# A planned attention and gated-unit kernel: new planner costs, reciprocal and product apart, products of two taps also on GpSimd

## The chip, the cores and the metric

The kernel runs on one core of a Trainium2 chip. The core has five engines that run side by side: TensorE (PE in the tables, its weight loads PEld), VectorE (DVE), ScalarE (ACT), GpSimd (POOL), and SyncE (SP), which here issues all transfers. Each engine works its own queue in order. Matmul results land in PSUM, eight banks; GpSimd's operands in this kernel all lie in SBUF. The metric is the device time of one launch in microseconds.

## What is computed

Eight batches of causal attention with a learned decay (8 heads, 576 positions, 64 per head), and on their result a gated linear unit with a causal convolution of five taps as its gate (conv_w is 5 x 512):

```python
scores = scale * np.matmul(q, k.transpose(0, 1, 3, 2))
s_pos = np.maximum(s, 0.0)
cum = np.cumsum(s_pos, axis=-1)
bias = -(cum[:, :, :, None] - cum[:, :, None, :])
scores = np.where(causal, -1000000000.0, scores + np.minimum(bias, 0.0))
...
attn = attn / (np.sum(attn, axis=-1, keepdims=True) + 1e-09)
return np.matmul(attn, v).astype(np.float32)
...
x = np.ascontiguousarray(attn_out.transpose(0, 2, 1, 3)).reshape(B, S, H * D)
...
K = conv_w.shape[0]
...
for k in range(K):
    gate_pre += conv_w[k][None, None, :] * xp[:, k:k + S, :]
gate = 1.0 / (1.0 + np.exp(-gate_pre))
val = x @ w_val
return (gate * val @ w_out).astype(np.float32)
```

## The kernel before, in words

The work is cut into 32 pieces `n`, four pairs of heads in each of eight batches; a pair of heads is also a block of 128 channels of the gated unit. For one piece:

- q and k are loaded (SP), cast to bf16 (the tiles qb and kb), transposed (PE, L524) and copied out of PSUM (QKT, L528, ACT or DVE). The last 64 positions of all heads go a way of their own (tail, tailb, L513, L516).
- V is multiplied by its decay weight w (Vp, L495), with a column of w beside it that later gives the sum of the row.
- Scores in three steps (PE, L533), each followed by an exp on ACT over 128x1024 (P, L559); the diagonal blocks of the first step are masked on POOL (L565), the last block apart (L545, L570).
- The product with V (PE, L580), a reciprocal of the sums (DVE, L586) and the normalisation (DVE, L587) give xn, which PE transposes (L595). An evacuation (L599, ACT or DVE) makes xT in SBUF.
- The convolution of this block: a first product, x times the weight of tap 0 (L395 on ACT, L397 on DVE or POOL), then four taps on DVE (L609), each adding a shifted product to gp in place, 575, 574, 573 and 572 columns wide. DVE and ACT read x from PSUM, POOL reads xT. A tanh (ACT, L614) ends it.
- Once the four xT blocks of a batch are there, PE makes val in halves of 288 columns (L621), DVE multiplies it into the gate (glu, L627), PE multiplies with w_out (L633), ACT or DVE copies the result out of PSUM (ot, L638), and SP stores it.

No order is written out. Every step is handed to a planner (`Plan`) with its engine, a duration, a due time made from the table `DUE`, and what it needs, takes and gives back (PSUM banks, and a few SBUF buffers: three P, two gp, six th, three ot, three qkf). Where more than one engine can do a step, a digit in the table `CHOICE` says which. `run` then plays the engines against each other with these durations: whenever an engine is free, it starts the ready step with the lowest due time. The order in which steps start is the order in which they are emitted, and so the order of every queue. A result is taken to reach another engine 0.2 us after its step ends (`LAG`), and its own engine at once:

```python
for o in after[t["n"]]:
    o["at"] = max(o["at"], t["done"] + (self.LAG if o["eng"] != e else 0.0))
```

A last step counts whether all reciprocals were in range (`check_recs`, `count`); if not, a general path would run. It does not here.

Of the kernel before, what the change touches and what calls it, by code (L numbers as in the profile page):

```python
# [2 lines left out]

# [201 lines left out]
def pcol(kb, qb):  # L205
    if kb == qb:
        return kb * 128
    if qb == 4:
# [13 lines left out]

DUE = dict(w=-9.02, lwv=-0.69, lwo=-0.63, cwv=-14.48, cwo=12.35, av=1.54, norm=-21.42, xt=-10.52, xe=-5.49,
           tap=4.19, dtap=-0.1, tanh=-21.1, val=6.51, dval=0.82, out=13.05, dout=0.32, oute=12.26,
           qt=-3.29, qe=62.47, tt=-0.65, te=-32.14, s4=-6.89, vp=-31.92, cast=41.14, lqk=-6.48,
           mask=-32.97, lv=-68.98)

STAY = (0.33, 20.6)  # L230

CHOICE = dict(cast="22212012",
              wts="00",
              te="10100110",
              qe="10010001000100000100100000000000",
              xe="01000110000001000110100110101101",
              tap0="10200210102212220121120122002000",
              oute="1010000010101000001000010000100000100000")


class Plan:

    LAG = 0.2
    SWITCH = 0.18

    def __init__(self, bufs):
# [14 lines left out]
    def run(self):  # L263
# [33 lines left out]
        while len(self.order) < len(self.tasks):  # L297
            started, later = False, []
            for e in engs:
# [50 lines left out]
                later.append(idle_at[e])  # L350
                started = True
                for o in after[t["n"]]:
                    o["at"] = max(o["at"], t["done"] + (self.LAG if o["eng"] != e else 0.0))
                    o["left"] -= 1
                    if o["left"] == 0:
                        ready[o["eng"]].append(o)
# [6 lines left out]
def main_path(ctx, tc, q, k, v, s, moe_w_val, moe_conv_w, moe_w_out, out, okcnt):  # L363
# [53 lines left out]
    xns = two("xn", [128, NKB, 512], BF16)  # L417
    xTs = two("xT", [128, 4, S], BF16)
    glus = two("glu", [128, 4, S], BF16)
    sp = one.tile([64, S], FP32, name="sp")  # L420
    cum = one.tile([64, S], FP32, name="cum")
    chalf = one.tile([64, 1], FP32, name="chalf")
# [35 lines left out]
    for m, (nm, src, dst, sc) in enumerate((("wv", moe_w_val, wv, 1.0), ("wo", moe_w_out, wo, 0.5))):  # L458
        def load(nm=nm, src=src):
            wt = slot[nm] = work("qkf", nm, [128, 4, DM], FP32)  # L460
            nc.sync.dma_start(out=wt, in_=src.rearrange("(c p) d -> p c d", c=4))
        t = add("SP", 3.6, DUE["l" + nm], load, take=[("qkf", nm)])
# [110 lines left out]
    def av(n, hh):  # L573
        b, p = divmod(n, 4)
        ps = slot["av", n] = pair(("av", n))
        for qb in range(NKB):
            for kb in range(qb + 1):
# [2 lines left out]
                nc.tensor.matmul(ps[:, hh, qb * 65:qb * 65 + 65], lhsT, Vps[b % 2][:, kb, 2 * p + hh, :],  # L580
                                 start=(kb == 0), stop=(kb == qb))

    def norm(n):
        b, p = divmod(n, 4)
        pv = slot["av", n][:, :, 0:NKB * 65].rearrange("t h (g d) -> t h g d", d=65)
        nc.vector.reciprocal(recs[:, n], pv[:, :, :, 64])  # L586
        nc.vector.tensor_tensor(xns[b % 2][:, :, p * 128:(p + 1) * 128].rearrange("t g (h d) -> t h g d", h=2),  # L587
                                pv[:, :, :, 0:64], recs[:, n].unsqueeze(3).to_broadcast([128, 2, NKB, 64]), ALU.mult)

# [7 lines left out]
    def x_evac(e, n):  # L597
        b, p = divmod(n, 4)
        copy[e](xTs[b % 2][:, p, :], slot["x", n])  # L599

    def tap0(e, n):
        b, c = divmod(n, 4)
        scaled(e, slot["g", n], xTs[b % 2][:, c, :] if e == "POOL" else slot["x", n], cwT[:, c, 4:5])

    def tap(n, sh):

# [36 lines left out]
    for b in range(B):  # L643
# [1 line left out]
        old = lambda name: [T.get((name, b - 2, i)) for i in range(4)]  # L645

        if b == 0:
            t_tl = add("SP", 1.6, -8.4, lambda: load_tail(0))
            t_tail = T["tailc", 0] = add("DVE", 0.45, -6, lambda: nc.vector.tensor_copy(tailbs[0], tails[0]), [t_tl])
            for p in range(4):  # L650
                for wh in range(2):
                    def ld(p=p, wh=wh):
                        f = slot["f", 0, wh, p] = one.tile([128, 2, 256], FP32, name=f"first{p}{wh}")
                        dma_qk(0, wh, HP[p], f)
                    t = add("SP", 0.95, -8.5 + 0.5 * p + wh * 0.01, ld)
                    T["cast", 0, wh, p] = add(("DVE", "ACT", "POOL"), (0.32, 0.5, 0.8), p - 9, lambda e, p=p, wh=wh: cast_qk(
                        copy[e], 0, wh, HP[p], slot["f", 0, wh, p]), [t], pick=("cast", 2 * p + wh))
                t = add("SP", 1.4, -8.3 + 0.5 * p, lambda p=p: load_v_pair(p))
                T["vp", 0, p] = add("DVE", 0.85, p - 2, lambda p=p: vprime(nc.vector, 0, p), [t, t_w])
        else:  # L660
            fs = []
            for wh in range(2):
                def ld(b=b, wh=wh):
                    f = slot["f", b, wh] = work("qkf", (b, wh), [128, 8, 256], FP32)
                    dma_qk(b, wh, slice(0, 8), f)
                t = add("SP", 3.8, n0 + DUE["lqk"], ld, take=[("qkf", (b, wh))])
# [5 lines left out]
            t = add("SP", 1.6, n0 + DUE["lqk"] + 0.5, lambda b=b: load_tail(b), [T.get(("tailc", b - 2))])  # L672
            t_tail = T["tailc", b] = add("POOL", 0.7, n0 + DUE["cast"] + 0.3, lambda b=b: nc.gpsimd.tensor_copy(
                tailbs[b % 2], tails[b % 2]), [t, T.get(("tt", b - 2))])
            ts = [add("SP", 1.7, n0 + DUE["lv"] + i * 0.01, lambda b=b, i=i: load_v_block(b, i),
                      [T["vp", b - 1, p] for p in range(4)]) for i in range(NKB)]
            for p in range(4):
                T["vp", b, p] = add("POOL", 1.4, n0 + p + DUE["vp"], lambda b=b, p=p: vprime(nc.gpsimd, b, p),
                                    ts + [t_w, T.get(("av", b - 2, p))])

        old_s = ([T.get(("s4", b - 2, 3))] + [T.get(("s", n0 - 8 + p, i)) for p in range(4) for i in range(3)])
# [22 lines left out]
        for p in range(4):  # L704
            n = n0 + p
            es = []
            for i in range(3):
                take = [("pair", ("s", n, i))] + ([("P", n)] if i == 0 else [])
                t = T["s", n, i] = add("PE", 0.26, n + 0.3 * i, lambda n=n, i=i: scores(n, i),
                                       [T["qe", b, p], t_te if i else None, T.get(("s", n, i - 1)), T.get(("s", n - 1, 2))],  # L710
                                       take=take, mode="R")
                t = add("ACT", 0.905, n + 0.3 * i, lambda n=n, i=i: exps(n, i), [t], give=[("pair", ("s", n, i))])
                es += [t] if i else [add("POOL", 0.58, n + DUE["mask"] + 0.01 * hh, lambda n=n, hh=hh: mask(n, hh), [t])
                                     for hh in range(2)]
# [10 lines left out]
            t = T["tap0", n] = add(("ACT", "DVE", "POOL"), (0.63, 0.73, 1.55), n + DUE["tap"],  # L725
                                   lambda e, n=n: tap0(e, n), [t, t_cw], pick=("tap0", n))
# [16 lines left out]
        for i in range(NKB):  # L743
            hfs = [(0,), (0,), (0, 1), (1,), (1,)][i]
            t = T["out", b, i] = add("PE", 0.88, n0 + DUE["out"] + DUE["dout"] * i, lambda b=b, i=i: outp(b, i),
                                     [T["glu", n0 + c, hf] for c in range(4) for hf in hfs] + [t_wo],
                                     take=[("bank", ("o", b, i))])
            t = add(("ACT", "DVE"), (0.49, 0.6), n0 + DUE["oute"] + DUE["dout"] * i, lambda e, b=b, i=i: out_evac(e, b, i),
                    [t], take=[("ot", (b, i))], give=[("bank", ("o", b, i))], pick=("oute", 5 * b + i))
            add("SP", 0.95, n0 + DUE["oute"] + DUE["dout"] * i, lambda b=b, i=i: store(b, i), [t], give=[("ot", (b, i))])  # L750


    onec = one.tile([128, 1], FP32, name="onec")
# [78 lines left out]
```

## Time and profile before

| | |
|---|---|
| median of 3 runs | 228.57 us (228.2 to 228.89) |
| the profiled execution, its own time | 229.07 us |
| its span, first to last instruction | 227.2 us |
| mean granted TensorE clock | 0.985 |
| last tap of the convolution ends on DVE | 211.07 us |
| last copy to ot (ACT) starts | 221.26 us |
| bytes moved by DMA | 40.48 MB, mean 178 GB/s |

The profile tells of one execution. A line of a group has the source line, engine, operation, tiles (written <- read), shapes and count, then busy time and the mean duration of one in ns, then the idle time ahead of them and what ended it. A line of a wait has who waited for what, total us, count and longest. A line of the timeline has start, duration (of a merged run from its first start to its last end), engine, line and operation. A table by stretch has for PE, PEld, DVE, ACT and POOL the busy time in the stretch and the count.

### The profile page before, as it was taken

To read this page: it belongs to the slowest core of one execution; us is meant where nothing else is said; L and a number is where in the kernel's file an instruction comes from. 1 tells how busy PE (TensorE), PEld (TensorE's weight loads), DVE (VectorE), ACT (ScalarE), POOL (GpSimd) and SP (SyncE) were. 2 spreads that over 40 slices of the span, in tenths; PEclk is the share of its full clock that TensorE was granted. 3 is DMA by queue.
4 is the path that set the end of the run, shared out by engine and by line. 5 is a ranking of instruction groups with operands and counts; after the bars stand their busy time and mean duration, and the time that the engine had idled before them with its cause. 6 is when DMAs were issued, how large, how long until landed. Compare 5 with 4: busy or idle time off the path is not lost. (4 is left out here: it accounts for less than half of the span.)

```text
span 227.2 us, 5999 instructions
## 1 busy us (share of the span) xinstructions
PE 174.9 (77%) x2392; PEld 117.6 (52%) x2411; DVE 192.5 (85%) x319; ACT 176.2 (78%) x229; POOL 138.6 (61%) x154
## 2 busy tenths in 40 slices
PE   0777667768576987798877988896998999999750
PEld 0555453455443664467545654675566555656320
DVE  3546989699999597999999899999999999999900
ACT  2395989954598599985999979899999799966330
POOL 5374574599264995799987876885945775200000
PEclk9999996999999999999999999999999999999996
DMA  4999889999996299907994683159229123034351
GB/s 137 245 278 305 245 160 258 315 228 207 312 307 166 60 196 364 301 12 173 233 346 178 137 246 114 41 130 153 92 95 220 50 83 94 3 132 157 128 190 35
DMA packets 69230, 40.48 MB, mean 178 GB/s; under 512 B 47109, under 2 KB 63493, under 8 KB 69194
## 3 DMA queue, kind: packets, MB, share of 16 engines
q1 hardware_dynamic: 69194, 40.01, 66.7%
q8 instruction: 21, 0.34, 0.7%
q14 instruction: 15, 0.12, 0.2%
HBM read 30.57 MB, written 9.44 MB: 176 GB/s over the span
## 5 line engine op out<-in xcount | busy, mean ns | idle before, releaser
L609 DVE SCALAR_TENSOR_TENSOR gp<-banks,cwT,gp 128x575 f32<-128x575 bf16 (+3 forms) x128 | 103.5, 812 | 3.2 <-ACT gp L395 0.3
L559 ACT ACTIVATE P<-banks 128x1024 bf16<-128x1024 f32 x96 | 95.1, 1030 | 11.7 <-PE banks L533 11.1
L565 POOL TENSOR_SCALAR_AFFINE_SELECT P<-P 128x512 bf16<-128x512 bf16 x64 | 40.4, 653 | 36.4 <-ACT P L559 36.2
L533 PE MATMUL banks<-QKT 64*128 64x128 bf16 (+4 forms) x576 | 39.5, 250 | 15.6 <-ACT P L559 6.3
L621 PE MATMUL banks<-xT,wv 128*128 128x288 bf16 x256 | 40.6, 288 | 5.0 <-DVE gp L609 3.0
L633 PE MATMUL banks<-wo,glu 128*128 128x512 bf16 x141 | 37.6, 379 | 4.7 <-DVE glu L627 1.1
L580 PE MATMUL banks<-Vp,P 128*128 128x65 bf16 x960 | 35.8, 196 | 2.8 <-POOL Vp L495 1.3
L580 PEld LDWEIGHTS <-P 128*128 128x128 bf16 x960 | 33.7, 99 | 6.4 <-issue 3.3
L533 PEld LDWEIGHTS <-QKT 64*128 64x128 bf16 x576 | 19.2, 97 | 31.7 <-issue 25.6
L495 POOL TENSOR_TENSOR Vp<-vst,w 128x650 bf16<-128x650 f32 x28 | 35.3, 1282 | 0.0
L621 PEld LDWEIGHTS <-wv 128*128 128x128 bf16 x256 | 23.0, 98 | 17.1 <-issue 10.3
L528 ACT COPY QKT<-banks 128x1024 bf16<-128x1024 bf16 x26 | 26.1, 1019 | 5.4 <-PE banks L524 5.1
L627 DVE SCALAR_TENSOR_TENSOR glu<-th,banks 128x288 bf16<-128x288 f32 x64 | 27.1, 447 | 3.2 <-PE banks L621 2.7
L614 ACT ACTIVATE th<-gp 128x576 f32<-128x576 f32 x32 | 22.1, 692 | 9.2 <-DVE gp L609 9.0
L587 DVE TENSOR_TENSOR xn<-banks,recs 128x640 bf16<-128x640 f32 x32 | 26.4, 825 | 1.1
L638 ACT COPY ot<-banks 128x512 f32<-128x512 f32 (+1 forms) x31 | 18.1, 587 | 9.6 <-PE banks L633 6.0
L397 POOL TENSOR_SCALAR gp<-xT,cwT 128x576 f32<-128x576 bf16 x12 | 20.7, 1725 | 7.3 <-ACT xT L599 4.1
L633 PEld LDWEIGHTS <-glu 128*128 128x128 bf16 x160 | 14.6, 97 | 18.2 <-issue 5.0
L595 PE MATMUL banks<-ident,xn 128*128 128x128 bf16 x160 | 14.6, 223 | 6.3 <-DVE gp L609 2.8
L595 PEld LDWEIGHTS <-xn 128*128 128x128 bf16 x160 | 9.9, 99 | 12.7 <-DVE xn L587 5.0
L524 PE MATMUL banks<-ident,qb 128*128 128x128 bf16 x128 | 13.2, 230 | 2.1 <-DVE glu L627 0.7
L485 POOL CAST qb<-qkf 128x2048 bf16<-128x2048 f32 x7 | 13.2, 1891 | 2.3 <-DMA qkf<-in_q_dram 2.3
(56 smaller groups left out, 148.5 us busy)
## 6 DMA issues: line engine op xcount, KB each, us to landing
out_dram<-ot SPq DMA_DIRECT2D x32, 256.0 KB, 2.1
qkf<-in_q_dram SPq DMA_DIRECT2D x7, 1024.0 KB, 9.3
qkf<-in_k_dram SPq DMA_DIRECT2D x7, 1024.0 KB, 8.8
vst<-in_v_dram SPq DMA_DIRECT2D x28, 256.0 KB, 5.0
vst<-in_v_dram SPq DMA_DIRECT2D x15, 128.0 KB, 4.5
first<-in_q_dram SPq DMA_DIRECT2D x4, 256.0 KB, 3.3
first<-in_k_dram SPq DMA_DIRECT2D x4, 256.0 KB, 3.5
tail<-in_q_dram SPq DMA_DIRECT2D x8, 128.0 KB, 8.8
```

Of the source, the lines that this page charges most:

```text
L495: eng.tensor_tensor(Vps[b % 2][:, :, h], vst[:, :, h], w[:, :, b * 8 + 2 * p:b * 8 + 2 * p + 2].unsqueeze(3).to_broadcast([128, NKB, 2, 65 ...
L528: copy[e](QKTs[b % 2][:, :, p, 0:512].rearrange("d w (x j) -> d w x j", j=4), slot["qt", b, p].rearrange("d w (j x) -> d w x j", j=4))
L533: nc.tensor.matmul(ps[:, hh, c0:c0 + nq], QKTs[b % 2][r, 1, p, k0:k0 + 128], QKTs[b % 2][r, 0, p, q0:q0 + nq], **kw)
L559: nc.scalar.activation(out=slot["Pt", n][:, :, step * 512:(step + 1) * 512], in_=slot["s", n, step], func=AF.Exp, scale=0.125)
L565: nc.gpsimd.affine_select(out=d, in_=d, pattern=[[0, 4], [1, 128]], compare_op=ALU.is_ge, fill=0.0, base=0, channel_multiplier=-1)
L580: nc.tensor.matmul(ps[:, hh, qb * 65:qb * 65 + 65], lhsT, Vps[b % 2][:, kb, 2 * p + hh, :], start=(kb == 0), stop=(kb == qb))
L587: nc.vector.tensor_tensor(xns[b % 2][:, :, p * 128:(p + 1) * 128].rearrange("t g (h d) -> t h g d", h=2), pv[:, :, :, 0:64], recs[:, n].un ...
L595: nc.tensor.transpose(pt[:, WIN[i]:WIN[i] + 128], xns[b % 2][:, i, p * 128:(p + 1) * 128], ident)
L609: nc.vector.scalar_tensor_tensor(gp[:, sh:S], x[:, 0:S - sh], cwT[:, c, 4 - sh:5 - sh], gp[:, sh:S], ALU.mult, ALU.add)
L621: nc.tensor.matmul(ps, wv[:, dc, c * 128:(c + 1) * 128], xTs[b % 2][:, dc, o:o + 288], start=(dc == 0), stop=(dc == 3))
L627: nc.vector.scalar_tensor_tensor(glus[b % 2][:, c, o], slot["t", n][:, o], 1.0, slot["v", n, hf], ALU.add, ALU.mult)
L633: nc.tensor.matmul(ps, glus[b % 2][:, c, WIN[i]:WIN[i] + 128], wo[:, c, :], start=(c == 0), stop=(c == 3))
```

## The change

Five things change in the code.

- The planner takes a result to reach a later step of the same engine 0.12 us after it was made, on DVE and ACT (`SAME`).
- Durations of transfers in the plan are replaced (for instance 3.6 by 2.8 for a weight matrix and 0.95 by 0.72 for a store), and a few of steps on POOL (1.55 by 1.13 for the first product, 1.4 by 1.25 for a Vp product).
- Reciprocal and normalisation are two steps, so that another step can stand between them.
- A first product on POOL is a product of two tensors (xT and a weight column repeated along the row) instead of one with a scalar.
- Tap 1 (575 columns) can go to POOL: a product into a new tile `tmp` and a sum into gp, two instructions in place of DVE's one.

The tables DUE, STAY and CHOICE have new numbers throughout. Counted by CHOICE: first products on ACT/DVE/POOL 12/8/12 before, 12/15/5 now; tap 1 on DVE/POOL 32/0 before, 22/10 now; QKT copies on DVE 6, now 7 (ACT 26, 25); copies to ot on DVE 9, now 11 (ACT 31, 29); the first batch's eight casts on DVE/ACT/POOL 1/2/5, now 2/4/2; the scaling of wo on DVE, now on ACT. Evacuations to xT stay 19 on DVE and 13 on ACT.

```diff
-CHOICE = dict(cast="22212012",
...
+CHOICE = dict(cast="11010221",
...
+              tap1="00100000000100010001000111100110",
...
     LAG = 0.2
+    SAME = 0.12
     SWITCH = 0.18
...
-                    o["at"] = max(o["at"], t["done"] + (self.LAG if o["eng"] != e else 0.0))
+                    o["at"] = max(o["at"], t["done"] + (self.LAG if o["eng"] != e else self.SAME if e in ("DVE", "ACT") else 0.0))
...
+    tmp = one.tile([128, S], FP32, name="tmp")
...
+    def recip(n):
+        pv = slot["av", n][:, :, 0:NKB * 65].rearrange("t h (g d) -> t h g d", d=65)
+        nc.vector.reciprocal(recs[:, n], pv[:, :, :, 64])
+
     def norm(n):
         b, p = divmod(n, 4)
         pv = slot["av", n][:, :, 0:NKB * 65].rearrange("t h (g d) -> t h g d", d=65)
-        nc.vector.reciprocal(recs[:, n], pv[:, :, :, 64])
...
+    def product(n, sh, out):
+        b, c = divmod(n, 4)
+        nc.gpsimd.tensor_tensor(out, xTs[b % 2][:, c, 0:S - sh], cwT[:, c, 4 - sh:5 - sh].to_broadcast([128, S - sh]),
+                                ALU.mult)
+
     def tap0(e, n):
-        b, c = divmod(n, 4)
-        scaled(e, slot["g", n], xTs[b % 2][:, c, :] if e == "POOL" else slot["x", n], cwT[:, c, 4:5])
+        if e == "POOL":
+            product(n, 0, slot["g", n])
+        else:
+            scaled(e, slot["g", n], slot["x", n], cwT[:, n % 4, 4:5])
+
+    def tap_either(e, n, sh):
+        if e == "DVE":
+            return tap(n, sh)
+        gp = slot["g", n]
+        product(n, sh, tmp[:, sh:S])
+        nc.gpsimd.tensor_tensor(gp[:, sh:S], gp[:, sh:S], tmp[:, sh:S], ALU.add)
...
-            t = T["norm", n] = add("DVE", 0.94, n + DUE["norm"], lambda n=n: norm(n), [t], give=[("pair", ("av", n))])
+            t = add("DVE", 0.13, n + DUE["norm"], lambda n=n: recip(n), [t])
+            t = T["norm", n] = add("DVE", 0.74, n + DUE["norm"], lambda n=n: norm(n), [t], give=[("pair", ("av", n))])
...
-            for sh in range(1, 5):
+            t = add(("DVE", "POOL"), (0.73, 2.25), n + DUE["tap"] + DUE["dtap"], lambda e, n=n: tap_either(e, n, 1), [t],
+                    pick=("tap1", n))
+            for sh in range(2, 5):
```

What the planner makes of it shows in the queues. On DVE, the first convolution of batch 0 (gp_300 before, gp_324 now) stood so before, in the order of issue:

```order
L586 RECIPROCAL recs<-banks 128x10
L587 TENSOR_TENSOR xn_95<-banks,recs 128x2x5x64
L609 SCALAR_TENSOR_TENSOR gp_300<-banks,cwT,gp_300 128x575
L609 SCALAR_TENSOR_TENSOR gp_300<-banks,cwT,gp_300 128x574
L609 SCALAR_TENSOR_TENSOR gp_300<-banks,cwT,gp_300 128x573
L609 SCALAR_TENSOR_TENSOR gp_300<-banks,cwT,gp_300 128x572
L586 RECIPROCAL recs<-banks 128x10
L587 TENSOR_TENSOR xn_95<-banks,recs 128x2x5x64
```

And the same convolution in DVE's queue of the changed kernel:

```order
L630 SCALAR_TENSOR_TENSOR gp_324<-banks,cwT,gp_324 128x575
L589 RECIPROCAL recs<-banks 128x10
L630 SCALAR_TENSOR_TENSOR gp_324<-banks,cwT,gp_324 128x574
L594 TENSOR_TENSOR xn_95<-banks,recs 128x2x5x64
L630 SCALAR_TENSOR_TENSOR gp_324<-banks,cwT,gp_324 128x573
L630 SCALAR_TENSOR_TENSOR gp_324<-banks,cwT,gp_324 128x572
L606 COPY xT_97<-banks 128x576
L589 RECIPROCAL recs<-banks 128x10
```

The reciprocal and the normalisation of the next piece now stand between the taps, where before the four taps followed each other and the normalisation followed its reciprocal.

On POOL, late in the program (the convolutions of batches 6 and 7; Vp is the next batch's V times its weight, AFFINE_SELECT the mask), the queue before:

```order
L397 TENSOR_SCALAR gp_2725<-xT_97,cwT 128x576
L565 AFFINE_SELECT P_2817<-P_2817 128x512 x2
L397 TENSOR_SCALAR gp_2834<-xT_97,cwT 128x576
L570 AFFINE_SELECT P_80<-P_80 128x8x64
L495 TENSOR_TENSOR Vp_94<-vst,w 128x5x130
L565 AFFINE_SELECT P_2937<-P_2937 128x512 x2
```

And now:

```order
L499 TENSOR_TENSOR Vp_94<-vst,w 128x5x130 x2
L610 TENSOR_TENSOR tmp<-xT_97,cwT 128x575
L624 TENSOR_TENSOR gp_2889<-gp_2889,tmp 128x575
L569 AFFINE_SELECT P_2944<-P_2944 128x512 x2
L610 TENSOR_TENSOR tmp<-xT_97,cwT 128x575
L624 TENSOR_TENSOR gp_2953<-gp_2953,tmp 128x575
L569 AFFINE_SELECT P_2999<-P_2999 128x512 x2
```

In place of a first product, POOL makes tap 1 here, in two instructions, for gp_2889 and gp_2953. DVE's queue at that place, from the first product of gp_2889 to its next tap on DVE:

```order
L400 TENSOR_SCALAR gp_2889<-banks,cwT 128x576
L589 RECIPROCAL recs<-banks 128x10
L648 SCALAR_TENSOR_TENSOR glu_100<-th_2562,banks 128x288
L594 TENSOR_TENSOR xn_95<-banks,recs 128x2x5x64
L648 SCALAR_TENSOR_TENSOR glu_100<-th_2662,banks 128x288 x2
L400 TENSOR_SCALAR gp_2953<-banks,cwT 128x576
L648 SCALAR_TENSOR_TENSOR glu_100<-th_2746,banks 128x288
L630 SCALAR_TENSOR_TENSOR gp_2889<-banks,cwT,gp_2889 128x574
```

Seven instructions stand between the two in the place where before tap 1 followed.

More of the change, by code (lines that the diff above doesn't have):

```diff
@@ L1 @@
 from contextlib import ExitStack
+from dataclasses import replace
 from functools import partial
@@ L221 @@
 NEG = -30000.0
[L225 to L230, printed above, removed]
-CHOICE = dict(cast="22212012",
[L233 to L238, printed above, removed]
+DUE = dict(w=-11.92, lwv=-1.5, lwo=1.13, cwv=25.09, cwo=26.57, av=0.18, norm=-6.55, xt=-31.82, xe=-95.88,
+           tap=5.87, dtap=-0.48, tanh=-86.25, val=8.05, dval=0.56, out=13.29, dout=0.66, oute=13.27,
+           qt=-3.85, qe=80.59, tt=-0.61, te=-73.02, s4=-74.03, vp=11.7, cast=54.26, lqk=-5.79, mask=-23.27,
+           lv=-12.75)
+STAY = (0.11, 48.1)
+CHOICE = dict(cast="11010221",
+              wts="01",
+              te="00001111",
+              qe="10100010000100000100100000100000",
+              xe="00100010001000011001001101110011",
+              tap0="10110212110112011010001121102000",
+              tap1="00100000000100010001000111100110",
+              oute="1001001110000100011000000101000000010000")
 class Plan:
     LAG = 0.2
+    SAME = 0.12
     SWITCH = 0.18
@@ L461, in load @@
             nc.sync.dma_start(out=wt, in_=src.rearrange("(c p) d -> p c d", c=4))
-        t = add("SP", 3.6, DUE["l" + nm], load, take=[("qkf", nm)])
+        t = add("SP", 2.8, DUE["l" + nm], load, take=[("qkf", nm)])
         t_wvo.append(add(("DVE", "ACT"), (1.35, 1.8), DUE["c" + nm], lambda e, nm=nm, dst=dst, sc=sc: scaled(
@@ L647, in main_path @@
         if b == 0:
-            t_tl = add("SP", 1.6, -8.4, lambda: load_tail(0))
+            t_tl = add("SP", 1.45, -8.4, lambda: load_tail(0))
             t_tail = T["tailc", 0] = add("DVE", 0.45, -6, lambda: nc.vector.tensor_copy(tailbs[0], tails[0]), [t_tl])
@@ L654, in ld @@
                         dma_qk(0, wh, HP[p], f)
-                    t = add("SP", 0.95, -8.5 + 0.5 * p + wh * 0.01, ld)
+                    t = add("SP", 0.82, -8.5 + 0.5 * p + wh * 0.01, ld)
                     T["cast", 0, wh, p] = add(("DVE", "ACT", "POOL"), (0.32, 0.5, 0.8), p - 9, lambda e, p=p, wh=wh: cast_qk(
                         copy[e], 0, wh, HP[p], slot["f", 0, wh, p]), [t], pick=("cast", 2 * p + wh))
-                t = add("SP", 1.4, -8.3 + 0.5 * p, lambda p=p: load_v_pair(p))
+                t = add("SP", 1.45, -8.3 + 0.5 * p, lambda p=p: load_v_pair(p))
                 T["vp", 0, p] = add("DVE", 0.85, p - 2, lambda p=p: vprime(nc.vector, 0, p), [t, t_w])
@@ L665, in ld @@
                     dma_qk(b, wh, slice(0, 8), f)
-                t = add("SP", 3.8, n0 + DUE["lqk"], ld, take=[("qkf", (b, wh))])
+                t = add("SP", 3.25, n0 + DUE["lqk"], ld, take=[("qkf", (b, wh))])
                 c = add("POOL", 1.95, n0 + DUE["cast"], lambda b=b, wh=wh: cast_qk(
@@ L671, in main_path @@
                     T["cast", b, wh, p] = c
-            t = add("SP", 1.6, n0 + DUE["lqk"] + 0.5, lambda b=b: load_tail(b), [T.get(("tailc", b - 2))])
+            t = add("SP", 1.45, n0 + DUE["lqk"] + 0.5, lambda b=b: load_tail(b), [T.get(("tailc", b - 2))])
             t_tail = T["tailc", b] = add("POOL", 0.7, n0 + DUE["cast"] + 0.3, lambda b=b: nc.gpsimd.tensor_copy(
                 tailbs[b % 2], tails[b % 2]), [t, T.get(("tt", b - 2))])
-            ts = [add("SP", 1.7, n0 + DUE["lv"] + i * 0.01, lambda b=b, i=i: load_v_block(b, i),
+            ts = [add("SP", 1.45, n0 + DUE["lv"] + i * 0.01, lambda b=b, i=i: load_v_block(b, i),
                       [T["vp", b - 1, p] for p in range(4)]) for i in range(NKB)]
             for p in range(4):
-                T["vp", b, p] = add("POOL", 1.4, n0 + p + DUE["vp"], lambda b=b, p=p: vprime(nc.gpsimd, b, p),
+                T["vp", b, p] = add("POOL", 1.25, n0 + p + DUE["vp"], lambda b=b, p=p: vprime(nc.gpsimd, b, p),
                                     ts + [t_w, T.get(("av", b - 2, p))])
@@ L712, in main_path @@
                 t = add("ACT", 0.905, n + 0.3 * i, lambda n=n, i=i: exps(n, i), [t], give=[("pair", ("s", n, i))])
-                es += [t] if i else [add("POOL", 0.58, n + DUE["mask"] + 0.01 * hh, lambda n=n, hh=hh: mask(n, hh), [t])
+                es += [t] if i else [add("POOL", 0.6, n + DUE["mask"] + 0.01 * hh, lambda n=n, hh=hh: mask(n, hh), [t])
                                      for hh in range(2)]
@@ L724, in main_path @@
                                  pick=("xe", n))
-            t = T["tap0", n] = add(("ACT", "DVE", "POOL"), (0.63, 0.73, 1.55), n + DUE["tap"],
+            t = T["tap0", n] = add(("ACT", "DVE", "POOL"), (0.63, 0.725, 1.13), n + DUE["tap"],
                                    lambda e, n=n: tap0(e, n), [t, t_cw], pick=("tap0", n))
-            for sh in range(1, 5):
+            t = add(("DVE", "POOL"), (0.73, 2.25), n + DUE["tap"] + DUE["dtap"], lambda e, n=n: tap_either(e, n, 1), [t],
+                    pick=("tap1", n))
+            for sh in range(2, 5):
                 t = add("DVE", 0.73, n + DUE["tap"] + sh * DUE["dtap"], lambda n=n, sh=sh: tap(n, sh), [t],
@@ L749, in main_path @@
                     [t], take=[("ot", (b, i))], give=[("bank", ("o", b, i))], pick=("oute", 5 * b + i))
-            add("SP", 0.95, n0 + DUE["oute"] + DUE["dout"] * i, lambda b=b, i=i: store(b, i), [t], give=[("ot", (b, i))])
+            add("SP", 0.72, n0 + DUE["oute"] + DUE["dout"] * i, lambda b=b, i=i: store(b, i), [t], give=[("ot", (b, i))])
     onec = one.tile([128, 1], FP32, name="onec")
```

## Prediction

> **What bounds the kernel now.** I read the page first: the span, the busy times and the slices.
>
> ```profile
> span 227.2 us, 5999 instructions
> PE 174.9 (77%) x2392; PEld 117.6 (52%) x2411; DVE 192.5 (85%) x319; ACT 176.2 (78%) x229; POOL 138.6 (61%) x154
> DVE  3546989699999597999999899999999999999900
> ```
>
> VectorE (DVE) is the fullest engine, and its slices show that the 85% is a mean of a thin start, a dip near slices 13 to 15, an end without work, and full slices between. So I asked next for the busy time by stage.
>
> ```profile
> 30.00:90.00 60.00, 44.05 (x633) 29.76 (x638) 53.20 (x85) 46.70 (x59) 40.45 (x43) 0.97 0.93 232
> 90.00:210.00 120.00, 104.87 (x1467) 70.50 (x1479) 116.10 (x195) 106.80 (x139) 80.99 (x81) 1.00 0.53 144
> ```
>
> The columns are PE, PEld, DVE, ACT and POOL busy, then clock and DMA. From 90 to 210 us DVE works 116.1 of 120 us. What ended its idle time says whether anybody keeps it waiting, first from 30 to 90 us, then from 90 to 210 us:
>
> ```profile
> DVE glu L627 <- PE banks L621: 2.5, 5, 0.8
> DVE recs L586 <- PE banks L580: 1.9, 2, 1.4
> DVE xT L599 <- PE banks L595: 0.5, 1, 0.5
> DVE glu L627 <- ACT P L559: 0.4, 1, 0.4
> DVE gp L609 <- ACT gp L395: 0.3, 1, 0.3
> ```
>
> ```profile
> DVE recs L586 <- PE banks L580: 0.9, 2, 0.5
> DVE gp L609 <- POOL gp L397: 0.3, 1, 0.3
> DVE glu L627 <- PE banks L621: 0.2, 1, 0.2
> DVE xT L599 <- PE banks L595: 0.2, 1, 0.2
> ```
>
> Each line ends with the total in us, the number of waits and the longest. DVE waits 5.6 us in the first 60, and 1.6 us in the 120 after them. There its own queue sets the end: a microsecond taken out of it there ends the kernel a microsecond earlier, until somebody else is late.
>
> The rest of DVE's loss lies between its own instructions. Its timeline inside that stretch (start, duration, operation):
>
> ```profile
> 157.79 0.45 DVE L627 SCALAR_TENSOR_TENSOR glu<-th,banks 128x288 bf16<-128x288 f32 x1
> 158.15 0.81 DVE L609 SCALAR_TENSOR_TENSOR gp<-banks,cwT,gp 128x573 f32<-128x573 bf16 x1
> 158.88 0.21 DVE L586 RECIPROCAL recs<-banks 128x10 f32<-128x10 f32 x1
> 159.12 0.82 DVE L587 TENSOR_TENSOR xn<-banks,recs 128x640 bf16<-128x640 f32 x1
> 159.87 0.45 DVE L599 COPY xT<-banks 128x576 bf16<-128x576 bf16 x1
> 160.23 0.80 DVE L609 SCALAR_TENSOR_TENSOR gp<-banks,cwT,gp 128x572 f32<-128x572 bf16 x1
> 160.95 0.45 DVE L627 SCALAR_TENSOR_TENSOR glu<-th,banks 128x288 bf16<-128x288 f32 x1
> 161.31 1.66 DVE L609 SCALAR_TENSOR_TENSOR gp<-banks,cwT,gp 128x575 f32<-128x575 bf16 x2
> 162.89 0.45 DVE L627 SCALAR_TENSOR_TENSOR glu<-th,banks 128x288 bf16<-128x288 f32 x1
> ```
>
> A tap (0.81) at 158.15 is followed by an unrelated reciprocal 0.73 later, before the tap has ended: about 0.08 of each duration overlaps the next instruction. Two taps of one chain take 1.66 together, so the second starts 1.66 - 0.81 = 0.85 after the first: it reads what the first writes. A product (L587) starts 0.24 behind the reciprocal that it reads, where 0.21 - 0.08 = 0.13 would do. **A neighbour that needs the result just made costs 0.12 us** (0.85 - 0.73; 0.24 - 0.13 gives 0.11).
>
> **The change, part by part.** Durations by group:
>
> ```profile
> L609 DVE SCALAR_TENSOR_TENSOR gp<-banks,cwT,gp 128x575 f32<-128x575 bf16 (+3 forms) x128 | 103.5, 812 | 3.2 <-ACT gp L395 0.3
> L397 DVE TENSOR_SCALAR gp<-banks,cwT 128x576 f32<-128x576 bf16 x8 | 6.5, 809 | 0.0
> L397 POOL TENSOR_SCALAR gp<-xT,cwT 128x576 f32<-128x576 bf16 x12 | 20.7, 1725 | 7.3 <-ACT xT L599 4.1
> L495 POOL TENSOR_TENSOR Vp<-vst,w 128x650 bf16<-128x650 f32 x28 | 35.3, 1282 | 0.0
> L528 DVE COPY QKT<-banks 128x1024 bf16<-128x1024 bf16 x6 | 7.3, 1218 | 0.4 <-ACT P L559 0.4
> L528 ACT COPY QKT<-banks 128x1024 bf16<-128x1024 bf16 x26 | 26.1, 1019 | 5.4 <-PE banks L524 5.1
> L638 DVE COPY ot<-banks 128x512 f32<-128x512 f32 x8 | 5.4, 680 | 0.0
> L638 ACT COPY ot<-banks 128x512 f32<-128x512 f32 x24 | 14.0, 588 | 6.8 <-PE banks L633 6.0 <-DMA out_dram<-ot 0.8
> L397 DVE TENSOR_SCALAR wo<-qkf 128x2048 bf16<-128x2048 f32 x1 | 1.6, 1645 | 0.0
> L485 DVE CAST kb<-first 128x512 bf16<-128x512 f32 x1 | 0.7, 661 | 0.3 <-DMA first<-in_k_dram 0.3
> L485 ACT CAST kb<-first 128x512 bf16<-128x512 f32 x1 | 0.6, 609 | 0.0
> ```
>
> *Order on DVE.* Counted over DVE's whole queue, before has 103 neighbours of which the second needs the first's result (68 tap behind tap, 3 tap behind first product, 32 product behind reciprocal); the changed queue has 27 (17, 2 and 8). The 76 others have a glu piece (0.36 from start to start), a reciprocal or a tap of another chain between them, which fills the 0.12. 76 x 0.12 = **-9.1 us**.
>
> *Work moved.* On DVE, each duration less the 0.08 of overlap: ten taps go to GpSimd, -10 x 0.73 = -7.3; seven first products come from it, +7 x 0.73 = +5.1; scaling wo goes to ACT, -1.6; one more QKT copy +1.1; two more output copies +1.2; one more first cast +0.6. Sum **-0.9**. DVE loses 10.0 us in all.
>
> ACT gets two first casts (2 x 0.5) and wo (between 1.0, the 1024-wide copy, and 2.0, twice that; I take 1.8), and gives one QKT copy (-0.9) and two output copies (-1.0): +0.9. Most of it stands in the first third, where ACT works 46.7 of 60 us; without that slack it would cost its 0.9.
>
> POOL gives twelve first products (-20.7) and three first casts (-2.4, at about 0.8), and gets five products and ten pairs of product and sum, 25 instructions. No row shows these. The nearest has two inputs from SBUF too, 1.28 for 650 columns, so 1.14 for 576; the other end is the one-input row, 1.725, which writes f32 as these do. I take 1.14, as the operation is the same: 28.5, POOL +5.4, to 144 us. With 1.725 it is 43.1, POOL 159 us, and each pair 3.45 instead of 2.28. Neither fills POOL; what it can cost is delay, a rival below.
>
> *New wait.* In ten chains DVE's second tap (128x574) now waits for POOL's sum; behind it in DVE's queue stand glu pieces, for whose banks PE waits. At the late place shown with the change, DVE has for gp_2889 between its first product and that tap four glu pieces (4 x 0.36), a reciprocal (0.13), a normalisation (0.75) and another first product (0.73), 3.0 us, against 2.28: no cost at 1.14, about 0.5 a chain at 1.725 (3.45 - 3.0).
>
> *Start and end.* The first pair's casts go from POOL to ACT, which can bring the first exp up to 1 us forward; later pairs wait for their loads, in the same order on SP. I take 0, with 1 us of gain as the other end. The load of wv passes the tail loads of the next batch on SP; these have a whole batch of work as cover, and I price it at 0 (up to 1 us if it is needed sooner). The final drain hangs on the last tap and on stores, which keep their sizes.
>
> *What is late next.* ACT, in the tightest stretch:
>
> ```profile
> 110.00:200.00 90.00, 78.03 (x1141) 52.96 (x1150) 87.14 (x148) 83.80 (x108) 62.78 (x65) 1.00 0.51 136
> 110.00:120.00 10.00, 7.78 (x90) 4.71 (x89) 9.86 (x15) 9.80 (x14) 8.52 (x9) 1.00 1.03 321
> ```
>
> The 10.0 us lie over some 187 us, so 4.8 of them in these 90, leaving 85.2 for 83.8 of ACT: 98%, the fullest that any row shows (9.80 of 10), while the stretch holds 93% now. I put the sustainable share between, at 96%: 83.8 / 0.96 = 87.3, so **+2.1** comes back. Net -10.0 + 2.1 = -7.9. The profiled execution took 229.07 us (span 227.2 and 1.9 around it) and would take 221.2, its span 219.3; the median shown, 228.57, is 0.5 lower, so the forecast is **220.7**.
>
> [...] The Trainium skill, Perfetto Trace Analysis, section "Optimizing Scalar/DVE Operations", warns that GpSimd and DVE share a read port, so that moving work between them might not help; by it the ten taps' 7.3 us would partly return. Here a tap lasts 0.81 with POOL 80.99 of 120 us busy, and the same 0.81 after 200 us, where POOL has no work left:
>
> ```profile
> 203.73 0.81 DVE L609 SCALAR_TENSOR_TENSOR gp<-banks,cwT,gp 128x575 f32<-128x575 bf16 x1
> 200.00:210.00 10.00, 9.79 (x64) 5.61 (x62) 9.79 (x16) 6.47 (x12) 0.00 (x0) 1.00 0.45 159
> ```
>
> **Rivals.**
> *All of it is kept.* ACT's work moves forward into the first third, where it has 13.3 us of slack, and nothing comes back: 218.6. If the order also halves DVE's 5.6 us of waits from 30 to 90 us: 215.8. For it: one order planned with truer costs; against: ACT at 98%.
> *New waits take the backlog's place.* DVE waits little after 90 us because work is piled up before it. Without the pile it could wait as from 30 to 90 us: 5.6 per 60, or 11.2 instead of 1.6 in 120. At three quarters of that rate 8.4 - 1.6 = +6.8 comes back: 225.4; at half 223.4, at the whole 228.2. Against: the early waits belong to the change from batch 0 to batch 1.
> *The change does not do what it says.* If a neighbour that needs no result costs as much as one that does, -0.9 is left: 227.7; the timeline's 0.73 against 0.85 denies it. If GpSimd's work slows DVE by what DVE gave away, 7.3 returns: 228.0; the equal tap durations deny it. [...]
> *Slower: GpSimd holds the chains.* At 1.725 an instruction each pair ends 1.17 later, and it queues behind a Vp product (1.28) or a mask that waits for an exp. If DVE stalls 1.17 for it in each of ten chains, on its second tap and with everything behind that, the time is 220.7 + 11.7 = 232.4. It decides from 0.79 a chain, where the 7.9 are gone. Against: DVE waited 0.3 in all for POOL's first products, and about 3 us of cover.
>
> **How the numbers follow.** Forecast 220.7 (219 to 222.5): 0.45. All kept (215.5 to 219): 0.24. New waits (222.5 to 228.2): 0.18. No effect of order, or slowed by GpSimd: 0.05. Slower: 0.08. From 215.5 to 226.5 the range leaves out the last two, 0.04 of the new waits and 0.02 below: 0.19. About 0.3% (0.7 us) can be told from no change: faster is 0.45 + 0.24 + 0.16 + 0.03 = 0.88; within it 0.05 (0.02 of the new waits, 0.02 of the third case, 0.01 of a milder GpSimd stall); slower 0.07.
>
> **What would show it.** DVE busy near 185 us (0.08 of each 0.12 counted as busy: 192.5 - 76 x 0.08 - 0.9 = 185.5); unrelated neighbours 0.73 apart, few merged rows of several taps; ACT near 9.6 of 10 from 110 to 200 us; POOL's products 1.14. I am wrong if DVE's waits from 90 us on exceed 4 us (new waits), if they name POOL with more than 1 us a chain (slower), or if a tap behind a stranger still starts 0.85 after the one before it.

## The result, and the profile after

The changed kernel takes 214.68 us (median of 4 runs, 213.75 to 215.21), the kernel before 228.73 beside it: a ratio of 0.9362 (worked out from all the runs, not from the two medians), 95% interval 0.9288 to 0.9437. The forecast was 220.7, range 215.5 to 226.5. The direction came out, and the main term of the sum; the gain is 14.05 us in place of 7.9, and the time lies 0.8 us under the range. The granted TensorE clock was lower than before, 0.955 after 0.985, so the gain isn't the clock's. The page of the changed kernel, span, busy times and DVE's slices:

```profile
span 213.5 us, 6047 instructions
...
PE 175.3 (82%) x2411; PEld 119.0 (56%) x2411; DVE 182.8 (86%) x319; ACT 175.8 (82%) x229; POOL 144.9 (68%) x164
...
DVE  3639886989998999998999999999989889999700
```

DVE is as full as before, and has 9.7 us less busy time. Its timeline in the full stretch shows how (start, duration, operation):

```profile
109.71 0.21 DVE L589 RECIPROCAL recs<-banks 128x10 f32<-128x10 f32 x1
109.84 0.75 DVE L630 SCALAR_TENSOR_TENSOR gp<-banks,cwT,gp 128x572 f32<-128x572 bf16 x1
110.51 0.81 DVE L594 TENSOR_TENSOR xn<-banks,recs 128x640 bf16<-128x640 f32 x1
111.24 0.21 DVE L589 RECIPROCAL recs<-banks 128x10 f32<-128x10 f32 x1
111.48 0.82 DVE L594 TENSOR_TENSOR xn<-banks,recs 128x640 bf16<-128x640 f32 x1
...
121.81 0.81 DVE L630 SCALAR_TENSOR_TENSOR gp<-banks,cwT,gp 128x572 f32<-128x572 bf16 x1
122.53 0.45 DVE L648 SCALAR_TENSOR_TENSOR glu<-th,banks 128x288 bf16<-128x288 f32 x1
122.89 0.81 DVE L630 SCALAR_TENSOR_TENSOR gp<-banks,cwT,gp 128x575 f32<-128x575 bf16 x1
123.61 0.44 DVE L648 SCALAR_TENSOR_TENSOR glu<-th,banks 128x288 bf16<-128x288 f32 x1
123.98 0.81 DVE L630 SCALAR_TENSOR_TENSOR gp<-banks,cwT,gp 128x574 f32<-128x574 bf16 x1
```

At 111.24 a reciprocal still has its reader behind it: 0.24. At 109.84 a tap starts 0.13 behind a reciprocal, and the reader is no longer held. From 121.81 on, taps and glu pieces alternate, 0.72 and 0.36 apart. Where DVE still waits, over the whole kernel, the four largest, and then from 90 us on alone:

```profile
DVE Vp L499 <- DMA vst<-in_v_dram: 4.4, 3, 1.9
DVE gp L630 <- POOL gp L624: 3.8, 5, 1.8
DVE recs L589 <- PE banks L584: 3.7, 6, 1.0
DVE sp L438 <- DMA sp<-in_s_dram: 3.4, 1, 3.4
```

```profile
DVE gp L630 <- POOL gp L624: 2.0, 4, 0.6
DVE ot L659 <- PE banks L654: 1.1, 1, 1.1
DVE recs L589 <- PE banks L584: 0.7, 2, 0.5
DVE xT L606 <- PE banks L602: 0.3, 1, 0.3
```

GpSimd's sums (L624) are the largest new wait, 3.8 us in five of ten chains. The wait for the loads of V has grown from 2.3 to 4.4, and from 90 us on DVE waits 4.1 us where it waited 2.0. From 30 to 90 us:

```profile
30.00:90.00 60.00, 49.60 (x706) 34.14 (x703) 56.05 (x95) 52.96 (x66) 48.06 (x49) 0.91 1.03 252
```

ACT, fourth of the busy times, did 46.70 us of work in these 60 before, and does 52.96 now. In the stretch that the forecast took as the tightest it does less, 79.20 us in place of 83.80:

```profile
110.00:200.00 90.00, 84.22 (x1110) 56.04 (x1108) 86.91 (x157) 79.20 (x107) 63.24 (x65) 1.00 0.45 118
```

For what follows, DVE's *work* is the time to the end of its last instruction less its idle gaps of 0.1 us and more, and those gaps are its *waits*. The difference of the spans, 227.2 - 213.5 = 13.7 us, then divides into

| | before | changed | |
|---|---|---|---|
| DVE's work | 196.5 | 184.1 | -12.4 |
| waits in the first 30 us | 12.1 | 10.4 | -1.7 |
| waits from 30 to 90 us | 5.7 | 3.7 | -2.0 |
| waits from 90 us on | 2.0 | 4.1 | +2.1 |
| from DVE's end to the end | 10.8 | 11.1 | +0.3 |

### The profile page after: what moved, and what is told of

The parts are those of the page before. It is cut to its first block, busy times and chain, and to the rows that moved or that the text cites. A ratio compares the mean times of both kernels' runs of the same rounds, so it can differ in the third digit from the quotient of the medians.

```text
span 213.5 us, 6047 instructions
## 1 busy us (share of the span) xinstructions
PE 175.3 (82%) x2411; PEld 119.0 (56%) x2411; DVE 182.8 (86%) x319; ACT 175.8 (82%) x229; POOL 144.9 (68%) x164
## 5 line engine op out<-in xcount | busy, mean ns | idle before, releaser
L630 DVE SCALAR_TENSOR_TENSOR gp<-banks,cwT,gp 128x573 f32<-128x573 bf16 (+3 forms) x118 | 94.2, 803 | 4.9 <-POOL gp L624 3.8
L569 POOL TENSOR_SCALAR_AFFINE_SELECT P<-P 128x512 bf16<-128x512 bf16 x64 | 39.8, 641 | 20.6 <-ACT P L563 20.5
L537 PE MATMUL banks<-QKT 64*128 64x128 bf16 (+4 forms) x576 | 38.8, 249 | 11.6 <-ACT P L563 4.2
L642 PE MATMUL banks<-xT,wv 128*128 128x288 bf16 x256 | 40.9, 294 | 2.6 <-ACT QKT L532 0.9
L654 PE MATMUL banks<-wo,glu 128*128 128x512 bf16 x160 | 39.6, 379 | 1.3 <-DVE xn L594 0.6
L584 PE MATMUL banks<-Vp,P 128*128 128x65 bf16 x960 | 37.2, 199 | 1.8 <-ACT P L563 0.8
L584 PEld LDWEIGHTS <-P 128*128 128x128 bf16 x960 | 35.4, 101 | 5.6 <-issue 1.4
L635 ACT ACTIVATE th<-gp 128x576 f32<-128x576 f32 x32 | 22.8, 712 | 4.4 <-DVE gp L630 3.9
L659 ACT COPY ot<-banks 128x512 f32<-128x512 f32 (+1 forms) x29 | 17.1, 591 | 10.6 <-PE banks L654 6.9
L624 POOL TENSOR_TENSOR gp<-gp,tmp 128x575 f32<-128x575 f32 x10 | 14.0, 1405 | 0.8
L610 POOL TENSOR_TENSOR tmp<-xT,cwT 128x575 f32<-128x575 bf16 x10 | 12.4, 1242 | 2.5 <-DVE xT L606 2.4
```

What stands on the lines that cost most here:

```text
L537: nc.tensor.matmul(ps[:, hh, c0:c0 + nq], QKTs[b % 2][r, 1, p, k0:k0 + 128], QKTs[b % 2][r, 0, p, q0:q0 + nq], **kw)
L569: nc.gpsimd.affine_select(out=d, in_=d, pattern=[[0, 4], [1, 128]], compare_op=ALU.is_ge, fill=0.0, base=0, channel_multiplier=-1)
L630: nc.vector.scalar_tensor_tensor(gp[:, sh:S], x[:, 0:S - sh], cwT[:, c, 4 - sh:5 - sh], gp[:, sh:S], ALU.mult, ALU.add)
L635: nc.scalar.activation(out=th, in_=slot["g", n], func=AF.Tanh, scale=0.5)
L642: nc.tensor.matmul(ps, wv[:, dc, c * 128:(c + 1) * 128], xTs[b % 2][:, dc, o:o + 288], start=(dc == 0), stop=(dc == 3))
L654: nc.tensor.matmul(ps, glus[b % 2][:, c, WIN[i]:WIN[i] + 128], wo[:, c, :], start=(c == 0), stop=(c == 3))
```

## The experiments

All times are medians of 4 to 10 runs beside runs of the kernel before on the same chip, whose medians lay between 227.5 and 230.5. The changed kernel itself was run again only beside x11 (as x12, 214.57); the other runs are set against its 214.68 from another set of runs, so that a difference of about 1 us decides little. Two questions stood: why more came than forecast, and what carries it. In the table, time, work and waits are in us; work and waits are DVE's, from the profiled execution.

| | time | work | waits |
|---|---|---|---|
| before | 228.73 | 196.5 | 19.9 |
| changed | 214.68 | 184.1 | 18.3 |
| x1_joined | 217.36 | 188.7 | 16.3 |
| x2_dve_load | 222.54 | 194.8 | 15.1 |
| x3_act_load | 219.86 | 185.3 | 22.3 |
| x6_tap1_dve | 215.74 | 190.4 | 12.2 |
| x4_same0 | 238.61 | 194.7 | 31.9 |
| x7_old_tables | 228.41 | 186.4 | 26.9 |
| x5_old_dma | 243.16 | 190.6 | 40.9 |
| x8_old_casts | 215.13 | 183.6 | 19.4 |
| x9_parted_before | 248.77 | 189.1 | 48.2 |
| x10_taps_together | 229.44 | 194.4 | 23.5 |
| x11_one_back | 212.77 | 184.9 | 14.8 |
| x12_again | 214.57 | 184.3 | 18.2 |

### What a microsecond on an engine is worth

**x1_joined**: the reciprocal is emitted with its reader again.

```diff
     def recip(n):
-        pv = slot["av", n][:, :, 0:NKB * 65].rearrange("t h (g d) -> t h g d", d=65)
-        nc.vector.reciprocal(recs[:, n], pv[:, :, :, 64])
+        pass
...
     def norm(n):
...
+        nc.vector.reciprocal(recs[:, n], pv[:, :, :, 64])
```

> The changed kernel with reciprocal and normalisation emitted together again, nothing else moved: 33 more neighbours on DVE that need the result just made (64 in place of 31). Theory A (DVE's queue sets the end, and an instruction between reciprocal and normalisation saves the 0.12 and is itself 0.05 shorter): 33 x 0.12 + 24 x 0.05 = 5.2 us more DVE work, 3.5 to 5.5 us longer. Theory B (the gain beyond the forecast came from waits that the new tables removed, DVE's occupation counts only in part): under 2.5 us longer.

The work grew by 4.6, near the 5.2, but 2.0 of it went into waits that DVE had anyway: 2.7 us longer, between the two theories.

**x2_dve_load**: `nc.vector.tensor_copy(spare, x)` ahead of each last tap. The spare copies are in no output.

> The changed kernel with one spare copy of x out of PSUM (128x576, 0.365 from start to start) on DVE in each of the 32 pieces, ahead of the last tap; 11.7 us of DVE work added, less 0.7 for six neighbours that it parts. Theory A (DVE sets the end): 8 to 11 us longer. Theory B (other engines' waits set the end as well, a queue with 18 us of idle time takes some): 3 to 7 us longer.

Work +10.7, waits -3.2, time +7.9: about three quarters of what is put on DVE shows. That lies between the two theories, just short of A.

**x3_act_load**: `nc.scalar.copy(spare[:, 1, :], spare[:, 0, :])`, 320 columns, behind each third exp, in no output either.

> The changed kernel with one spare copy of 320 columns (estimate 0.33 from start to start, from 0.48 for 512) on ACT behind the third exp of each piece; 10.6 us of ACT work added. Theory A (ACT follows DVE and its work moves forward when there is room): at most 4 us longer. The forecast's step (ACT can't hold more than about 96% of the tight stretch): nearly all of it, 8 to 11 us longer.

ACT's work grew by 10.9 (176.4 to 187.3, counted as DVE's), the time by 5.2. Half of it shows: ACT is neither free, as theory A had it, nor at its ceiling, as the forecast had it, and the time lies between the two. DVE's waits grew by 4.0.

**x6_tap1_dve**: `tap_either` always returns `tap(n, sh)`.

> The changed kernel with the ten tap 1 that GpSimd makes given back to DVE at their place in the order; DVE +10 x 0.73 = 7.3 us, POOL -25.5 us, and 3.8 us of DVE waits for POOL's sums gone. Theory A: 7.3 less the 3.8 = 3.5, to 7.3 us longer. Theory B (GpSimd's taps give back in waits what they take from DVE): within 2 us of the changed kernel.

Work +6.3, waits -6.1, time +1.1: theory B. The five waits for POOL are gone, and others with them. Ten taps on GpSimd are worth about 1 us, little more than such a comparison can tell; they are not where the gain is.

### Costs, tables, order

**x4_same0**: one number in the planner, which then plans anew.

```diff
-    SAME = 0.12
+    SAME = 0.0
```

> The changed kernel with the planner's latency of a result on its own engine set back to 0 (SAME = 0.0), all tables and costs new: the order changes, and DVE has 107 neighbours that need the result just made, as many as before. Theory A (the latency in the plan carries most of the gain): 76 x 0.12 + 1 = 10 us more DVE work, of which, by the spare work on DVE (8 us of time for 11 of work), 6 to 9 us longer than the changed kernel, 221 to 224. Rival (the new tables and costs carry it): within 3 us of the changed kernel, under 218.

**x7_old_tables**: DUE, STAY and CHOICE of before, `tap1` all 0, in the changed code.

> The changed code and costs with the old tables (due times and choices; tap 1 all on DVE): 39 neighbours that need the result just made. Theory A: 69 x 0.12 = 8.3 us less DVE work than before at the same distribution of work, 5 to 9 us shorter than before, 219 to 223. Rival (tables have to be found for the latency, or the order runs into new waits): less than 3 us shorter than before, 225 or more.

**x5_old_dma**: the plan's transfer times of before.

```diff
-        t = add("SP", 2.8, DUE["l" + nm], load, take=[("qkf", nm)])
+        t = add("SP", 3.6, DUE["l" + nm], load, take=[("qkf", nm)])
...
-                t = add("SP", 3.25, n0 + DUE["lqk"], ld, take=[("qkf", (b, wh))])
+                t = add("SP", 3.8, n0 + DUE["lqk"], ld, take=[("qkf", (b, wh))])
```

> The changed kernel with the plan's transfer times as before (3.6, 3.8, 1.6, 1.7, 0.95 and so on): the order changes, 50 neighbours that need the result just made in place of 31. Theory A (transfer times matter only through the order on DVE): 19 x 0.12 = 2.3 us of DVE work, 1 to 3 us longer than the changed kernel. Rival (the true transfer times carry a good part of the gain): 5 us longer or more.

In x4 the time missed both theories' numbers; in x7 and x5 it came as the rival had it, in x5 far beyond. All three show one thing. Without the latency DVE's work is back at 194.7, as expected, but its waits grow by 13.6 too, and the kernel is slower than before. With the old tables, DVE has 10.1 us less work than before, more than I had counted, but 7.0 us more waits, and the kernel ends 13.1 us after DVE's last work, not 10.8: the ratio to the kernel before is 1.005 (1.0013 to 1.0087). Its waits, the three largest:

```profile
DVE recs L589 <- PE banks L584: 7.5, 9, 1.9
DVE sp L438 <- DMA sp<-in_s_dram: 3.6, 1, 3.6
DVE glu L648 <- PE banks L642: 2.7, 3, 1.5
```

So costs and tables belong together: costs of one kernel with tables of the other, either way round, put 7 to 23 us of waits into DVE's queue. Whether a transfer time by itself matters, x5 can't say, as it moved the whole order. Nor were these waits parted from the TensorE clock, which was lower in these runs (0.916 in x4, 0.928 in x5, 0.939 in x7, against 0.955); whether it is a cause of them or follows from them is open.

**x10_taps_together** and **x9_parted_before** leave costs and tables alone and edit the finished order on DVE. The first moves a reader up behind what it reads, past one step; the second, in the kernel before, moves one of the next four steps between two such neighbours, with reciprocal and product as two steps.

```diff
     plan.total = plan.run()
+    join()
```

The edit of x10 rests on these lines (a, c and b are three steps in a row on DVE):

```python
...
a, c, b = dve[i:i + 3]
pc, pb = where(c), where(b)
if (a["n"] in reads(b) and not b["take"]
        and not any(u["n"] in reads(b) for u in o[pc:pb])):
    o.insert(pc, o.pop(pb))
...
```

> The changed kernel with its own tables, costs and engines; only in DVE's queue, where one step lies between a result and its reader, the reader goes first: 101 such neighbours in place of 31. Theory A: 70 x 0.12 + 24 x 0.05 = 9.6 us more DVE work, of which 0.55 to 0.73 shows in the time (spare work on DVE, reciprocals joined): 5 to 7 us longer than the changed kernel, 219.5 to 222. Rival (the tables alone make the gain): under 2.5 us longer.

> The kernel before with its own tables, costs and engines; only in DVE's queue, where a neighbour reads the result just made, one of the next four steps is put between (reciprocal and product as two steps): 24 such neighbours in place of 108. Theory A (the 0.12 a neighbour is what DVE's bound stretch gives up): 84 x 0.12 + 27 x 0.05 = 11.4 us less DVE work, at some waits of steps put forward: 6 to 11 us shorter than before, 218 to 223. Rival (without tables found for it the order runs into new waits, as with the old tables): less than 3 us shorter, 226 or more.

Putting the neighbours together takes the whole gain away: 229.44, where the kernel before took 225.71 to 231.01 beside it. Work +10.3, near the 9.6 worked out; but the waits grew too, +5.2, and so the loss is twice what theory A allowed. That each step which a reader passed now comes some 0.7 us later may be the reason; it was not shown by itself. In its timeline the chain stands in one merged row again, and two waits of 0.5 follow:

```profile
102.54 2.50 DVE L630 SCALAR_TENSOR_TENSOR gp<-banks,cwT,gp 128x574 f32<-128x574 bf16 x3
104.95 0.44 DVE L648 SCALAR_TENSOR_TENSOR glu<-th,banks 128x288 bf16<-128x288 f32 x1
105.93 0.46 DVE L606 COPY xT<-banks 128x576 bf16<-128x576 bf16 x1 [0.53 <-PE banks L602]
106.91 0.22 DVE L589 RECIPROCAL recs<-banks 128x10 f32<-128x10 f32 x1 [0.52 <-PE banks L584]
```

Parting them by hand in the old order is far worse than leaving them, 248.77. The work falls by 7.4; the waits grow by 28.3. The waits of that run, the three largest:

```profile
DVE recs L585 <- PE banks L580: 13.0, 12, 4.4
DVE glu L630 <- PE banks L624: 12.1, 15, 1.7
DVE xT L602 <- PE banks L598: 4.2, 7, 1.4
```

A step put forward to fill a gap of 0.12 may not be ready, and in an in-order queue everything behind it waits too. That holds for a part: matched with the old order, 14.7 of the 28.3 us have grown ahead of steps that now stand further forward, the rest ahead of others. The 0.12 shows in DVE's work in both runs; the time follows only where the order brings no new waits.

### The start, and a better version

**x8_old_casts**: the first eight casts on their old engines, order kept.

```diff
     def cast_qk(eng, b, which, hs, f):
+        if b == 0:
+            eng = copy[("POOL", "POOL", "POOL", "ACT", "POOL", "DVE", "ACT", "POOL")[hs.start + which]]
```

> The changed kernel with the first batch's eight casts on the engines of before (five on POOL, two on ACT, one on DVE), order kept. If DVE's shorter wait at the start (10.4 us idle in the first 30 us, 12.2 before) comes from these casts: 1.2 to 2 us longer than the changed kernel. If it comes from the order of the first pieces: within 0.7 us.

0.45 longer, within the runs' spread, with 10.9 us of waits in the first 30 us: the casts explain 0.5 of the 1.7 us at most. The order of the first pieces is left as the reason, not shown by itself.

The largest of the new waits stands at 33 us. DVE's timeline of the changed kernel there, and POOL's:

```profile
31.11 1.43 DVE L400 TENSOR_SCALAR wv<-qkf 128x2048 bf16<-128x2048 f32 x1
32.46 0.80 DVE L630 SCALAR_TENSOR_TENSOR gp<-banks,cwT,gp 128x572 f32<-128x572 bf16 x1
35.05 0.81 DVE L630 SCALAR_TENSOR_TENSOR gp<-banks,cwT,gp 128x574 f32<-128x574 bf16 x1 [1.79 <-POOL gp L624]
```

```profile
30.84 0.61 POOL L694 CAST tailb<-tail 128x512 bf16<-128x512 f32 x1 [2.89 <-DMA tail<-in_k_dram]
31.42 2.11 POOL L610 TENSOR_TENSOR tmp<-xT,cwT 128x575 f32<-128x575 bf16 x1
33.61 1.40 POOL L624 TENSOR_TENSOR gp<-gp,tmp 128x575 f32<-128x575 f32 x1
```

POOL waits 2.89 us for the tail load, which the load of wv now passes on SP; its product then takes 2.11 while DVE scales wv; DVE waits 1.79 for the sum. Most of the 2.89 isn't a later load, though. Before, the same cast stood so:

```profile
30.15 0.62 POOL L673 CAST tailb<-tail 128x512 bf16<-128x512 f32 x1
```

It now starts only 0.7 us later, while POOL is free for it at 27.96 in place of 30.21. New is that a tap stands behind it. **x11_one_back** gives this one tap back to DVE, order kept; **x12_again** is the changed kernel on the same chip.

```diff
     def tap_either(e, n, sh):
-        if e == "DVE":
+        if e == "DVE" or n == 2:
             return tap(n, sh)
```

> The changed kernel with tap 1 of the third piece (the first that GpSimd makes) on DVE, order kept. In the changed kernel's profile DVE waits 1.79 us for that sum at 33.3 us: POOL stood 2.89 us at the cast before it for the tail load, and the product took 2.11 in place of 1.14. On DVE the tap costs 0.73. If DVE's early waits reach the end: 0.5 to 1.1 us shorter than the changed kernel run beside it. If ACT and PE, which are late there too, set the pace: within 0.4 us.

> The changed kernel unaltered, on the same chip as the one before this, for comparison: 214 to 215.5.

212.77 us (212.12 to 213.46) against 214.57 (213.55 to 215.26), all six runs under all six: 1.8 us, more than expected. DVE's work +0.6, its waits -3.4: beside the 1.79, 1.6 elsewhere have gone. This version beats both kernels, at 0.9372 of the one before (0.9327 to 0.9416).

## Why the prediction was right, and where it was wrong

- *A neighbour that reads the result just made costs 0.12.* Right. Such rows still show 0.24 and 0.84, others 0.13 and 0.72; DVE's work grew by 4.6 us in x1 and by 10.3 in x10, near what the count of neighbours gives.
- *DVE's queue bounds the kernel, and a microsecond of its work is a microsecond of time.* Right in the first half alone. Of a microsecond put on DVE, 0.58 showed in x1, 0.74 in x2 and 0.17 in x6; in x10, where the order changed, more than one did.
- *DVE loses 10.0 us* (-9.1 by order, -0.9 by moved work). Too small: 12.4. An instruction between a reciprocal and its reader is mostly 0.05 shorter (0.75 at 109.84 beside 0.81), of which no row of before could tell; over the 24 places that is 0.9 (1.2, if all had it, as the expectations of x1 and x10 counted). The moved work came to an estimated -1.3, since the casts cost less than their row's 0.66 (0.42 each). The last 1.1 was not traced.
- *ACT gives 2.1 back.* This step failed, and it is the one that hid the outcome. I took ACT's work in the stretch from 110 to 200 us as fixed. It moved: ACT had done 74.7 us by 90 us where it had done 65.3 before, does 88% of that stretch and not 96%, and no wait of DVE from 90 us on names it. DVE's waits from 30 us on are 7.9 where they were 7.7. That this comes so near to nothing is partly luck: 2.1 us of new waits did come from 90 us on, half of them for GpSimd's sums, and 2.0 went between 30 and 90 us, for which the sum had no term. Nearest to it is the rival "all of it is kept" with shorter early waits, 215.8; I gave that rival 0.24. x3 shows that ACT's room has a limit: 10.9 us more on it cost 5.2.
- *The start costs and brings nothing.* Waits there fell by 1.7, more than the 1 us I allowed, and at most 0.5 of it by the casts, on which I had it rest (x8).
- *wv passing the tail loads is covered by a batch of work.* Near enough for the load itself, as POOL's cast comes 0.7 us later. What I did not price is the tap behind it: the cast, a product of 2.11 and the sum made DVE wait 1.79, and taking the tap back is worth 1.8 us (x11). No run puts the load back. Without this cost the time would lie further under the range.
- *Products on GpSimd at 1.14.* The product is 1.14 (1.24 in the mean, with the 2.11), the sum 1.40, so a pair is 2.55, not 2.28: inside the bounds. The slower rival needed 0.79 in each of ten chains; it was 3.8 in all. But I counted the ten taps as 7.3 us of relief, and x6 says that they are worth 1.1.
- *New waits take the backlog's place*, a rival at 0.18 (its time at half the rate is 222.6, not 223.4). It came in part: I had named more than 4 us of waits from 90 us on as a sign of it, and they are 4.1. With the old tables (x7) it is what happens. Nothing in the profile of before could tell how much it would be; the order could have been read further for it.
- Of the other signs, DVE's 185 us came out as 182.8; ACT's 9.6 of 10 from 110 to 200 us as 8.8.

Together: 2.4 of work, 1.9 of waits from 30 us on (2.1 forecast, 0.2 come) and 1.7 at the start, less 0.3 at the end, are 5.7 of the 5.8 us between a span of 219.3 and one of 213.5; the rest is rounding.

```profile
L630 DVE SCALAR_TENSOR_TENSOR gp<-banks,cwT,gp 128x573 f32<-128x573 bf16 (+3 forms) x118 | 94.2, 803 | 4.9 <-POOL gp L624 3.8
L624 POOL TENSOR_TENSOR gp<-gp,tmp 128x575 f32<-128x575 f32 x10 | 14.0, 1405 | 0.8
L610 POOL TENSOR_TENSOR tmp<-xT,cwT 128x575 f32<-128x575 bf16 x10 | 12.4, 1242 | 2.5 <-DVE xT L606 2.4
```

These groups of the changed kernel hold the durations named above.

## What to carry to other kernels

Measure the time from start to start for neighbours that depend on each other and for those that don't, and give a planner both: here the difference of 0.12 us, over some 76 places, is 9.1 of the 13.7 us by count. But an order is a whole: less work on the bounding engine is only kept if whatever stands between is ready, and in the three runs with a cost or a table of the other kernel it was not. When the bounding engine gets relief, ask whether the next engine's work can move to an earlier stretch before subtracting for it.

## What the hardware showed beside this

- An instruction on DVE between a reciprocal and its reader mostly lasts 0.05 us less, a tap 0.75 in place of 0.81, with 0.13 between the starts ahead of it. Of the 24 in the changed kernel, seven last 0.80 to 0.81. In all seven the reciprocal stands behind the earlier step of the same convolution (judged by the widths) and starts before that step has ended, as at 76.76 here; at 78.34 it stands behind a normalisation:

```profile
76.03 0.82 DVE L630 SCALAR_TENSOR_TENSOR gp<-banks,cwT,gp 128x575 f32<-128x575 bf16 x1
76.76 0.21 DVE L589 RECIPROCAL recs<-banks 128x10 f32<-128x10 f32 x1
76.89 0.81 DVE L630 SCALAR_TENSOR_TENSOR gp<-banks,cwT,gp 128x574 f32<-128x574 bf16 x1
77.61 0.81 DVE L594 TENSOR_TENSOR xn<-banks,recs 128x640 bf16<-128x640 f32 x1
78.34 0.21 DVE L589 RECIPROCAL recs<-banks 128x10 f32<-128x10 f32 x1
78.47 0.75 DVE L630 SCALAR_TENSOR_TENSOR gp<-banks,cwT,gp 128x573 f32<-128x573 bf16 x1
```

  I know no reason for the shorter time.
- GpSimd's in-place sum of two f32 tiles takes 1.40 us for 575 columns, its product of bf16 with a repeated f32 column 1.14 (all but one of 15), and the old form with one tensor and a scalar 1.725 for 576.
- One product took 2.11 us, and DVE's scaling of wv beside it 1.43 (1.217 before); the product was 2.11 there in x1, x2, x3 and x12 too. In x8 it starts after the scaling has ended, and the two take 1.14 and 1.22. The Trainium skill, Perfetto Trace Analysis, section "Optimizing Scalar/DVE Operations", says that GpSimd and DVE share a read port, which an operation of DVE on two ports holds alone; this one place agrees; the taps, which read x from PSUM, show nothing of it.
